# Two-layer transformer on one core: moving 32x32-square transposes of the MLP rows to VectorE

## The chip, the cores and the metric

The kernel runs on 1 core of one Trainium2 chip. The metric is device time in microseconds (us) of one launch; less is better. Engines are named as the profile names them: PE (TensorE, matrix multiply) with PEld (its weight loads), DVE (VectorE), ACT (ScalarE), POOL (GpSimd) and SP (the queue that issues most DMAs). Each engine works through its own instructions in order and waits on semaphores for the others.

## What is computed

Two equal layers, each an attention block and an MLP block, on one sequence of 2048 rows with 640 columns, all in fp32:

```python
x = x + A(layernorm(x))   # 32 heads of 20 columns: qkv = x @ wqkv, softmax(q k^T / sqrt(20)) v, then @ wo
x = x + B(layernorm(x))   # relu(x @ w1 + b1) ** 2 @ w2 + b2, with 1536 hidden columns
x = x + A(layernorm(x))
x = x + B(layernorm(x))
```

Each fp32 operand is split in a high part (rounded to PE's faster fp32r form) and a low part (the rest). A product is three matmuls: high x high, high x low, low x high (`THREE`, L284).

## The kernel before, in words

**Rows and blocks.** The 2048 rows are four blocks of 512 (`QB`), each block four row tiles of 128 rows x 640 columns. A matmul contracts over partitions, so the normalised rows must stand transposed: five tiles `xnT` of 128 columns (`k`) x 512 rows, high and low part side by side. Five tiles of 128 columns make the 640.

**How rows are transposed.** PE turns a 128x128 square by a matmul with the identity: twenty for a block, four into each of five PSUM banks. Then `split_to` (L265) makes the high part on ACT (L267, reads the bank) and the low part on DVE (L268), 128x512 each. This is done in `front` (L370, transposes at L385) for the attention's input and in `transposed` (L1037, transposes at L1042) for the MLP's.

**A layer.** `layer` (L1096) runs `qkv`, `attention`, then for each block `add_heads` (L1005: 8 chains of 15 matmuls with `wo`, each followed by a DVE add into the row tile, L1020), then for each block `mlp` (L1050).

**One MLP block.** `mlp` goes twice (`fh`) through the same two phases. The f phase has six hidden tiles: a chain of 15 matmuls of 128x512 on PE; relu with bias on ACT (L1065); the square on DVE (L1066); the split into `h` on ACT (L267) and DVE (L268). The y phase has eight chains (two column halves x four row tiles) of 18 matmuls of 128x320, each followed by a DVE add (L1085). The eight y chains need all six `h`. In the first f phase POOL also adds the bias `b2` to the four row tiles (L1072).

**What sets the order.** The order of each engine's instructions is the order in which the Python code issues them. Work for later is cut into generators, and `side()` (L1107), called after every chain, takes one step from the list `steps`:
- `normal_rows` (L1024) prepares the rows of the next block for `transposed`: one step of four loads on SP, four of statistics (`stats`, L250, DVE and two small POOL instructions, L258 and L259), four of `normalise` on DVE (L263).
- In an ordinary block these ten steps begin after six empty ones. `transposed` for the next block is called in the second y phase, after its third chain.
- For the first MLP block the ten steps are taken during the last `add_heads` block, and `transposed` follows it directly.
- In the last MLP block of the first layer the side steps are `ahead`: `second` (L1144), the `front` of the second layer's blocks 0, 1 and 2, three steps a call, from the first chain of the second f phase on; a `front` has 14 steps.

**Buffers.** Row tiles and the intermediate `r` share 11 buffers (`NX`), weights and `xnT`, `h` share 42 slots, PSUM has eight banks that `ps_all` hands out in turn, so PE can be eight chains ahead of whoever empties them.

Of the kernel before, what the change touches and what calls it, by code (L numbers as in the profile page):

```python
# [16 lines left out]
P = 128  # L17
# [7 lines left out]
QB = 512  # L25
# [14 lines left out]
def tile_layers(  # L40
# [221 lines left out]
    def normalise(eng, x, mv):  # L262
        eng.tensor_scalar(x, x, mv[:, 0:1], mv[:, 1:2], op0=ALU.subtract, op1=ALU.mult)  # L263
# [17 lines left out]
    def pool_lo(dst, a, b):  # L281
        nc.gpsimd.tensor_sub(dst, a, b)  # L282

    THREE = ((0, 0), (0, 1), (1, 0))  # L284

    def row_tile(src, r):
# [83 lines left out]
    def front(tb, x_src, bank):  # L370

        rows = [row_tile(x_src, tb * 4 + i) for i in range(4)]
        yield
        mvs = []
        for x in rows:
            mvs.append(stats(x))
            yield
        for x, mv in zip(rows, mvs):
            normalise(nc.vector, x, mv)
            yield  # L380
        res = []
        for k in range(KD):
            dst = bank("xt")
            for i in range(4):
                nc.tensor.transpose(  # L385
                    dst[:, i * P : (i + 1) * P], rows[i][:, k * P : (k + 1) * P], ident
                )
# [5 lines left out]
            yield  # L393

    def fronts(steps):

# [627 lines left out]
    def normal_rows(qb, x_src, res):  # L1024

        xs = [row_tile(x_src, qb * 4 + i) for i in range(4)]
        yield
        mvs = []
        for x in xs:
            mvs.append(stats(x))  # L1030
            yield
        for x, mv in zip(xs, mvs):
            normalise(nc.vector, x, mv)
            yield
        res.extend(xs)

    def transposed(xs):  # L1037
        xnt = []
        for k in range(KD):
            dst = ps_all("xt")  # L1040
            for i in range(4):
                nc.tensor.transpose(  # L1042
                    dst[:, i * P : (i + 1) * P], xs[i][:, k * P : (k + 1) * P], ident
                )
            t = slot([P, 2, QB], F32R, "xnT")
            split_to(t[:, 0, :], t[:, 1, :], dst)
            xnt.append(t)
        return xnt

    def mlp(qb, xnt, x_mid, x_dst, side, nxt):  # L1050

        xs, res = [], None
        for fh in range(2):
            hs = []
            for f in range(fh * 6, fh * 6 + 6):
                dst = ps_all("pu")
# [8 lines left out]
                nc.scalar.activation(r, dst, AF.Relu, bias=b1_t[:, f : f + 1])  # L1065
                nc.vector.tensor_mul(r, r, r)  # L1066
                h = slot([P, 2, QB], F32R, "h")
                split_to(h[:, 0, :], h[:, 1, :], r)
                hs.append(h)
                if fh == 0 and f in (1, 2, 3, 4):  # L1070
                    x = row_tile(x_mid, qb * 4 + f - 1)
                    nc.gpsimd.tensor_add(x, x, b2_t)  # L1072
                    xs.append(x)
                side()
            for hf in range(2):
                c = slice(hf * HALF, (hf + 1) * HALF)
                for i in range(4):
                    dst = ps_all("y")
                    chain(dst[:, :HALF], [
                        (hs[f % 6][:, hx, i * P : (i + 1) * P], w_2.piece(at_2(f, hw, hf)))  # L1080
                        for f in range(fh * 6, fh * 6 + 6)
                        for hx, hw in THREE
                    ])
                    x = xs[i]
                    nc.vector.tensor_add(x[:, c], dst[:, :HALF], x[:, c])  # L1085
                    if fh == 1 and hf == 1:
                        r0 = (qb * 4 + i) * P
                        dma(nc.sync, x_dst[r0 : r0 + P, :], x)
                    side()
                    if (fh, hf, i) == (1, 0, 2) and nxt:  # L1090
                        res = transposed(nxt)
            if fh == 0 and qb == NQB - 1:
                w_2.past(at_2(5, 1, 1))
        return res

    def layer(first, x_a, x_m, x_e, front_0, ahead):  # L1096
        qkv(first, x_a, front_0)
# [12 lines left out]

        def all_steps():
            while steps:
                side()

        for qb in range(NQB):
            if qb + 1 == NQB:
                rows = []
                norm = normal_rows(0, x_m, rows)
                steps.extend([lambda: next(norm, None)] * 10)
            add_heads(qb, x_a, x_m, xs, side)  # L1120
            for s in range(qb * 4, min(qb * 4 + 4, w_1.n)):
                w_1.load(s)
            if qb > 1:
                all_steps()
        w_o.drop()
        xnt = transposed(rows)
        for s in range(w_2.n):
            w_2.load(s)
        for qb in range(NQB):
            rows = []  # L1130
            if qb + 1 < NQB:
                norm = normal_rows(qb + 1, x_m, rows)
                steps.extend([None] * 6 + [lambda norm=norm: next(norm, None)] * 10)
            elif ahead:
                some = lambda: [next(ahead, None) for _ in range(3)]
                steps.extend([None] * 14 + [some] * 14)
            xnt = mlp(qb, xnt, x_m, x_e, side, rows if qb + 1 < NQB else None)
            if qb + 1 < NQB:
                all_steps()
        steps.clear()  # L1140
        w_1.drop()
        w_2.drop()

    def second():  # L1144

# [66 lines left out]
```

## Time and profile before

| what | value |
|---|---|
| median of the runs (lowest to highest) | 3760.36 us (3759.33 to 3761.38, 3 runs) |
| the profiled execution's own time | 3758.89 us |
| its span, first to last instruction | 3757.1 us |
| mean granted TensorE clock | 0.993 |
| PE busy | 3700.7 us, 98% of the span |
| DVE busy | 2788.9 us, 74% |
| ACT busy | 2554.5 us, 68% |
| POOL busy | 830.9 us, 22% |
| the eight MLP blocks | about 1537 to 1893 and 3409 to 3757 us of the span |

How to read it: busy time is an average over stages with different limits. In attention PE, DVE and ACT are all near full; in the MLP blocks the 40 slices of the page show DVE at four tenths and ACT at two. What a change in the MLP is worth is read there, from windows and timelines of that stretch, not from the averages.

### The profile page before, as it was taken

Reading aid. Unit: us, or ns where it says so; the run is one execution under the profiler, and the core shown is the slowest. Engines: PE = TensorE matmul, PEld = TensorE weight load, DVE = VectorE, ACT = ScalarE, POOL = GpSimd, SP = SyncE. Lnnn points to the kernel's source line nnn. Section 1 sums busy time; section 2 is a strip of 40 time slices with the busy share of each in tenths; the row PEclk is TensorE's granted clock in tenths of the full one; section 3 lists DMA queues with packets and bytes.
Section 4 is the critical chain, followed back from the end, with each engine's and each line's share of the span. In section 5 each row is a group of like instructions: output and inputs, shape, how many; then the busy total and the mean of one; then the engine's idle time right before and its main releaser. Section 6 shows DMA issues by size and latency. Waiting matters only on the chain.

```text
span 3757.1 us, 64225 instructions
## 1 busy us (share of the span) xinstructions
PE 3700.7 (98%) x23572; PEld 2121.8 (56%) x23572; DVE 2788.9 (74%) x4790; ACT 2554.5 (68%) x4887; POOL 830.9 (22%) x921
## 2 busy tenths in 40 slices
PE   7999999999999999999999999999999999999999
PEld 5667344333443336989866773344433344368998
DVE  7788999999999992444457879999999999814443
ACT  2454999999999995122214449999999999941211
POOL 6540234321112211111154201211221112101110
PEclk9999999999999999999999999999999999999999
DMA  7553554432212135511255543222222221365111
GB/s 223 185 205 133 130 155 148 138 104 67 65 48 60 44 93 192 222 43 43 95 168 182 160 141 83 77 67 64 70 73 56 54 54 43 99 217 191 43 46 39
DMA packets 258282, 405.87 MB, mean 108 GB/s; under 512 B 67828, under 2 KB 114676, under 8 KB 257968
## 3 DMA queue, kind: packets, MB, share of 16 engines
q1 hardware_dynamic: 257424, 400.06, 34.4%
q8 instruction: 186, 3.05, 0.3%
q10 hardware_dynamic: 544, 1.71, 0.2%
q14 instruction: 128, 1.05, 0.1%
HBM read 264.82 MB, written 136.81 MB: 107 GB/s over the span
## 4 chain that ended last, share of the span: by engine, by line
PE 92%; DMA 3%; DVE 2%; POOL 1%; ACT 1%; SPq 0%; issue 0%; ACTq 0%; DVEq 0%; POOLq 0%
PE banks L572 27%; PE banks L560 20%; PE banks L297 20%; PE banks L463 15%; PE banks L308 6%; PE banks L355 3%; DMA q<-d_qk 1%; DMA k<-d_qk 1%; PE banks L1042 0%; SPq L76 0%; DVE bst L255 0%; PE banks L385 0%; DVE h L268 0%; DVE r L1066 0%; POOL xnT L282 0%; DVE mx L484 0%
## 5 line engine op out<-in xcount | busy, mean ns | idle before, releaser
L567 ACT ACTIVATE e<-banks 128x512 f32<-128x512 f32 x4096 | 2113.9, 602 | 60.7 <-PE banks L560 4.4
L475 DVE TENSOR_REDUCE mx<-banks 128x1 f32<-128x512 f32 x2928 | 1839.4, 684 | 180.9 <-PE banks L463 112.8
L463 PE MATMUL banks<-k,q 60*128 60x512 f32 x3744 | 1153.2, 436 | 10.8 <-DMA q<-d_qk 7.8
L560 PE MATMUL banks<-q,k 62*128 62x512 f32 x4096 | 1151.7, 435 | 2.6 <-DVE mx L484 2.1
L572 PE MATMUL banks<-e,vg 128*32 128x512 f32 x8192 | 1092.1, 605 | 0.0
L560 PEld LDWEIGHTS banks<-q,k 62*128 62x128 f32 x4096 | 600.4, 185 | 701.2 <-ACT e L567 667.6
L463 PEld LDWEIGHTS banks<-k,q 60*128 60x128 f32 x3744 | 537.3, 185 | 337.3 <-DVE mx L475 204.2
L495 ACT ACTIVATE rl<-banks 128x512 f32<-128x512 f32 x352 | 191.6, 596 | 256.0 <-PE banks L463 255.9
L572 PEld LDWEIGHTS banks<-e,vg 128*32 128x32 f32 x8192 | 161.6, 108 | 358.5 <-issue 331.7
L297 PE MATMUL banks<-w,h 128*128 128x320 f32 x2304 | 352.7, 312 | 3.2 <-DVE h L268 2.7
L297 PEld LDWEIGHTS banks<-w,h 128*128 128x128 f32 x2304 | 340.8, 189 | 12.7 <-DVE h L268 6.9
L297 PE MATMUL banks<-xnT,w 128*128 128x512 f32 x1440 | 331.0, 390 | 0.0
L308 PE MATMUL banks<-xnT,wqk 128*128 128x512 f32 x1200 | 326.9, 416 | 1.1 <-POOL wqk L282 1.1
L1065 ACT ACTIVATE r<-banks,b_t 128x512 f32<-128x512 f32 x96 | 66.1, 689 | 381.1 <-PE banks L297 381.0
L505 DVE CUSTOM_DVE_ANT_0 rl<-banks,rl 128x512 f32<-128x512 f32 x352 | 229.2, 689 | 121.4 <-PE banks L463 116.3
L297 PEld LDWEIGHTS banks<-xnT,w 128*128 128x128 f32 x1440 | 270.1, 188 | 55.4
L484 DVE TENSOR_REDUCE mx<-banks 128x2 f32<-128x1024 f32 x232 | 279.6, 1221 | 25.6 <-PE banks L463 24.9
L308 PEld LDWEIGHTS banks<-xnT,wqk 128*128 128x128 f32 x1200 | 222.3, 195 | 87.4 <-issue 43.8
L616 POOL TENSOR_TENSOR few<-few,minus_t 128x16 f32<-128x16 f32 x62 | 179.9, 2902 | 226.3 <-DMA few<-d_s 223.0
L279 POOL CAST mr<-nt 128x32 fp32r<-128x32 f32 x64 | 13.5, 211 | 923.3 <-DVE nt L531 923.3
L1085 DVE TENSOR_TENSOR x<-banks,x 128x320 f32<-128x320 f32 x128 | 62.8, 491 | 200.8 <-PE banks L297 191.6
L627 POOL TENSOR_TENSOR o<-o 128x512 f32<-128x512 f32 x62 | 79.7, 1285 | 567.1 <-DMA o<-d_r 340.2
(73 smaller groups left out, 2000.9 us busy)
## 6 DMA issues: line engine op xcount, KB each, us to landing
q<-d_qk SPq DMA_DIRECT2D x756, 80.0 KB
d_qk<-ev SPq DMA_DIRECT2D x80, 512.0 KB
k<-d_qk SPq DMA_DIRECT2D x468, 80.0 KB
x<-d_x SPq DMA_DIRECT2D x96, 320.0 KB
d_o<-ot SPq DMA_DIRECT2D x248, 80.0 KB
ot<-d_o SPq DMA_DIRECT2D x38, 512.0 KB
d_v<-v SPq DMA_DIRECT2D x32, 512.0 KB
vg<-d_v SPq DMA_DIRECT2D x32, 512.0 KB
```

The source lines that it names most:

```text
L297: nc.tensor.matmul(dst, a, b, start=(n == 0), stop=(n == last))
L308: nc.tensor.matmul(dst, w_qk.piece(pos * 10 + hw * KD + k), xt_[tb][k][:, hx, :], start=(n == 0), stop=(n == 3 * KD - 1),)
L355: nc.tensor.matmul(dst[:, :HALF], xt_[tb][k][:, hx, i * P : (i + 1) * P], w_v.piece(k * 4 + hw * 2 + hf), start=(j == 0), stop=(j == 3 * K ...
L463: nc.tensor.matmul(dst, q_t[t][b : b + 60, p, sub * P : (sub + 1) * P], k_t[t // NQB, c][b : b + 60, p, :], start=True, stop=True,)
L475: nc.vector.tensor_reduce(maxima(t)[:, 2 * p + par, sub, c : c + 1], dst, axis=AX.X, op=ALU.max)
L484: nc.vector.tensor_reduce(maxima(t)[:, 2 * p : 2 * p + 2, sub, c], dst, axis=AX.X, op=ALU.max)
L495: nc.scalar.activation(res[par], dst[:, par, :], AF.Relu)
L505: nc.vector.tensor_tensor_reduce(out=r[par], in0=dst[:, par, :], in1=r[par], scale=1.0, scalar=LEAST, op0=ALU.add, op1=ALU.max, accum_out= ...
L560: nc.tensor.matmul(dst, k_t[t // NQB, kt // 4][b : b + 62, p, (kt % 4) * P : (kt % 4 + 1) * P], q_t[t][b : b + 62, p, :], start=True, stop ...
L567: nc.scalar.activation(es[p][:, par, :], dst, AF.Exp, scale=SCALE)
L572: nc.tensor.matmul(acc[32 * h : 32 * h + 32, :], v_t[t // NQB, kt // 8][:, kt % 8, 32 * h : 32 * h + 32], es[p][:, par, :], start=(kt == 0 ...
L616: nc.gpsimd.tensor_tensor(few, few, minus_t, op=ALU.pow)
```

## The change

Three things:

1. **Squares of 32 on DVE.** A new helper `turned` turns a 128x640 row tile into `y`, whose columns `k*128 ... k*128+127` are the transpose of the tile's k-th 128x128 square. It takes 16 `nc.vector.transpose` instructions; each reads 32 partitions x (5 x 32) elements and writes them, square by square, to 32 partitions x (5 x 32). It yields after eight and after sixteen. `parts` then makes the high part on ACT and the low part on POOL, in pieces of 128x128: five of each for a row tile. `transposed` and the fronts of the second layer's blocks 0 and 1 use these; the first layer's fronts and the second layer's blocks 2 and 3 stay on PE.
2. **Steps.** A block of `normal_rows` now has 14 steps instead of ten. For the first MLP block they begin one `add_heads` block earlier. `transposed` is called after the first chain of the second y phase instead of the third.
3. **The last block.** In the last MLP block of each layer, hidden tiles 0 to 3 of each half are squared on POOL and their low part is made there, instead of on DVE; tiles 4 and 5 stay.

```diff
+    def turned(x):
+        y = xtile("y")
+        view = y.rearrange("p (k t) -> p k t", k=KD)
+        src = x.rearrange("p (k c i) -> p c k i", k=KD, i=32)
+        for a in range(4):
+            for c in range(4):
+                nc.vector.transpose(
+                    view[32 * c : 32 * c + 32, :, 32 * a : 32 * a + 32],
+                    src[32 * a : 32 * a + 32, c],
+                )
+            if a % 2:
+                yield y
+
+    def parts(res, i, y):
+        for k, t in enumerate(res):
+            cols = slice(i * P, (i + 1) * P)
+            nc.scalar.copy(t[:, 0, cols], y[:, k * P : (k + 1) * P])
+            pool_lo(t[:, 1, cols], y[:, k * P : (k + 1) * P], t[:, 0, cols].bitcast(F32))
...
+    def front_turned(tb, x_src):
...
+        for i, mv in enumerate(mvs):
+            x = rows[i]
+            normalise(nc.vector, x, mv)
+            for y in turned(x):
+                yield
+            rows[i] = x = None
+            if not res:
+                res = [slot([P, 2, QB], F32R, "xnT") for _ in range(KD)]
+            parts(res, i, y)
+        xt_[tb] = res
+        yield
...
-        for x, mv in zip(xs, mvs):
-            normalise(nc.vector, x, mv)
-            yield
-        res.extend(xs)
-
-    def transposed(xs):
-        xnt = []
-        for k in range(KD):
-            dst = ps_all("xt")
-            for i in range(4):
-                nc.tensor.transpose(
-                    dst[:, i * P : (i + 1) * P], xs[i][:, k * P : (k + 1) * P], ident
-                )
-            t = slot([P, 2, QB], F32R, "xnT")
-            split_to(t[:, 0, :], t[:, 1, :], dst)
-            xnt.append(t)
+        for i, mv in enumerate(mvs):
+            normalise(nc.vector, xs[i], mv)
+            for y in turned(xs[i]):
+                yield
+            xs[i] = None
+            res.append(y)
+
+    def transposed(ys):
+        xnt = [slot([P, 2, QB], F32R, "xnT") for _ in range(KD)]
+        for i, y in enumerate(ys):
+            parts(xnt, i, y)
         return xnt
...
-                nc.vector.tensor_mul(r, r, r)
                 h = slot([P, 2, QB], F32R, "h")
-                split_to(h[:, 0, :], h[:, 1, :], r)
+                if qb < NQB - 1 or f % 6 > 3:
+                    nc.vector.tensor_mul(r, r, r)
+                    split_to(h[:, 0, :], h[:, 1, :], r)
+                else:
+                    nc.gpsimd.tensor_mul(r, r, r)
+                    nc.scalar.copy(h[:, 0, :], r)
+                    pool_lo(h[:, 1, :], r, h[:, 0, :].bitcast(F32))
...
-                    if (fh, hf, i) == (1, 0, 2) and nxt:
+                    if (fh, hf, i) == (1, 0, 0) and nxt:
...
-            if qb + 1 == NQB:
+            if qb + 2 == NQB:
...
-                steps.extend([lambda: next(norm, None)] * 10)
+                steps.extend([lambda: next(norm, None)] * 14)
...
-            if qb > 1:
+            if qb + 1 == NQB:
                 all_steps()
...
-                steps.extend([None] * 6 + [lambda norm=norm: next(norm, None)] * 10)
+                steps.extend([None] * 6 + [lambda norm=norm: next(norm, None)] * 14)
...
-        yield from front(0, d_x[1], ps_all)
-        for n, _ in enumerate(front(1, d_x[1], ps_all)):
+        yield from front_turned(0, d_x[1])
+        for n, _ in enumerate(front_turned(1, d_x[1])):
```

More of the change, by code (lines that the diff above doesn't have):

```diff
@@ L393, in front @@
             yield
+    def front_turned(tb, x_src):
+        rows = [row_tile(x_src, tb * 4 + i) for i in range(4)]
+        yield
+        mvs = []
+        for x in rows:
+            mvs.append(stats(x))
+            yield
+        res = []
+        for i, mv in enumerate(mvs):
[8 more added lines that the diff above has]
+        xt_[tb] = res
+        yield
     def fronts(steps):
@@ L1031, in normal_rows @@
             yield
-        for x, mv in zip(xs, mvs):
-            normalise(nc.vector, x, mv)
-            yield
-        res.extend(xs)
-    def transposed(xs):
-        xnt = []
-        for k in range(KD):
-            dst = ps_all("xt")
-            for i in range(4):
-                nc.tensor.transpose(
-                    dst[:, i * P : (i + 1) * P], xs[i][:, k * P : (k + 1) * P], ident
-                )
-            t = slot([P, 2, QB], F32R, "xnT")
-            split_to(t[:, 0, :], t[:, 1, :], dst)
-            xnt.append(t)
+        for i, mv in enumerate(mvs):
+            normalise(nc.vector, xs[i], mv)
+            for y in turned(xs[i]):
+                yield
+            xs[i] = None
[4 more added lines that the diff above has]
+            parts(xnt, i, y)
         return xnt
```

## Prediction

> **What bounds the kernel now.** I read the page's chain first, then windows over the MLP blocks, then the timelines of PE and DVE there.
>
> ```profile
> PE 92%; DMA 3%; DVE 2%; POOL 1%; ACT 1%; SPq 0%; issue 0%; ACTq 0%; DVEq 0%; POOLq 0%
> ```
>
> The chain that ends last is PE for 92% of the span. Whatever leaves PE there is time won; whatever makes PE wait is time lost. The windows (length, then busy time of PE, PEld, DVE, ACT, POOL, granted clock) show one ordinary block, its transposes, and the middle of the first layer's last block:
>
> ```profile
> 1611.00:1691.00 80.00, 79.63 (x439) 71.52 (x439) 34.06 (x57) 16.11 (x25) 10.93 (x12) 1.00 0.15 50
> 1691.00:1698.00 7.00, 7.00 (x55) 6.99 (x54) 2.83 (x6) 2.46 (x5) 0.00 (x0) 1.00 0.00 0
> 1843.00:1870.00 27.00, 24.88 (x117) 20.48 (x116) 17.80 (x36) 10.05 (x17) 3.89 (x8) 0.94 0.31 99
> ```
>
> An ordinary block leaves PE idle for 0.4 us of 80 while DVE has 46 us free, so moving transposes to DVE looks free. But the second f phase, where most of the new work goes, has to be read by itself. PE, the chain's piece for the transposes, then DVE:
>
> ```profile
> 1665.84 20.59 PE L297 MATMUL banks<-xnT,w 128*128 128x512 f32 x90
> 1686.27 2.94 PE L297 MATMUL banks<-w,h 128*128 128x320 f32 x17
> 1689.37 5.69 PE L297 MATMUL banks<-w,h 128*128 128x320 f32 x37 [0.16 <-DVE h L268]
> 1695.06 2.18 PE banks L1042 x20
> ```
>
> ```profile
> 1660.76 0.49 DVE L1085 TENSOR_TENSOR x<-banks,x 128x320 f32<-128x320 f32 x1 [1.11 <-PE banks L297]
> 1661.17 0.60 DVE L263 TENSOR_SCALAR x<-x,mv 128x640 f32<-128x640 f32 x1
> 1670.24 0.69 DVE L1066 TENSOR_TENSOR r<-r 128x512 f32<-128x512 f32 x1 [3.18 <-ACT r L1065]
> 1687.25 0.69 DVE L1066 TENSOR_TENSOR r<-r 128x512 f32<-128x512 f32 x1 [1.33 <-ACT r L1065]
> 1688.63 0.69 DVE L268 TENSOR_TENSOR h<-r,h 128x512 fp32r<-128x512 f32 x1 [0.69 <-ACT h L267]
> ```
>
> A hidden tile comes every 20.59/6 = 3.43 us. DVE holds 2.07 us of that in one piece (1687.25 to 1689.32: square, wait for ACT's copy, subtraction), leaving 1.36 us. Its last h lands at 1689.32, just as PE needs it: PE waits only 0.16 us. And the transposes that leave PE are worth just **2.18 us a block**.
>
> **The change part by part.** All hangs on T, the time from one 32x(5x32) transpose to the next. A block needs 64.
>
> ```profile
> L531 DVE STREAM_TRANSPOSE nt<-nm 128x32 f32<-128x32 f32 x64 | 13.6, 212 | 6.7 <-DVE nm L520 0.5
> L268 DVE TENSOR_TENSOR xnT<-banks,xnT 128x512 fp32r<-128x512 f32 x60 | 38.0, 685 | 13.5 <-ACT xnT L267 13.4
> 1536.05 3.08 DVE L268 TENSOR_TENSOR xnT<-banks,xnT 128x512 fp32r<-128x512 f32 x5 [1.09 <-ACT xnT L267]
> L171 ACT CAST wqk<-raw 128x128 fp32r<-128x128 f32 x2 | 0.6, 300 | 0.0
> L282 POOL TENSOR_TENSOR w<-raw,w 128x128 fp32r<-128x128 f32 x6 | 2.8, 460 | 0.2
> ```
>
> From this kernel's own rows: DVE's copy of a 128x320 bank into x takes 0.49 us and the 128x512 subtraction 0.685, so 192 elements cost 0.195 us, 1.02 ns each. The transpose of 32 elements takes 0.212 us: 0.18 fixed and 0.033 for elements. With 160 elements it is 0.18 + 0.163 = **0.345 us alone**. Five subtractions in a row took 3.08 us, (3.08 - 0.685)/4 = 0.60 apart: like neighbours overlap by 0.085 us, and all but 0.075 us of fixed cost can hide, so the lower estimate is 0.163 + 0.075 = **0.235 us**. Nothing shows less than 0.163 (elements alone) or excludes 0.48 (if each square of 32 is filled and emptied by itself, 0.18 - 0.033 + 10 x 0.033). I take 0.345: it is the nearest row, the same operation, taken whole, and each new transpose writes to other partitions than the one before, which the overlapping subtractions don't.
>
> The Trainium skill, "VectorE: DVE Perf Modes", section "Two Vector instructions with no wait between them", says that an instruction whose output starts in another group of 32 partitions than the last one starts only when all earlier ones have finished. The inner loop changes that group every time, so by it T is 0.345 and not 0.235; no row of this trace shows such a pair.
>
> *A. Six ordinary second f phases (blocks 0 to 2, both layers).* The changed order on DVE, from the sixth add of the first y phase (ends 1661.17 where the next instruction starts): four normalisations (0.61) and 64 transposes, with two adds (0.45) and six tiles (2.07) between: 2.44 + 64T + 0.90 + 12.42 = 15.8 + 64T. With 0.345 that is 37.8 us: the last h lands at 1699.0 instead of 1689.32, **9.7 us late**. DVE is busy throughout: it reaches tile 0's square at 1671.6, after 1670.24 when the relu was there. PE has finished the f phase at 1686.4 and stands in the first y chain; all later y chains are behind it in its order. Less 2.18 us of transposes: +7.5. Waiting costs more than the wait:
>
> ```profile
> 1874.07 0.33 PE L385 MATMUL banks<-ident,x 128*128 128x128 f32 x1 [1.84 <-DVE x L263]
> 1876.12 4.42 PE L297 MATMUL banks<-w,h 128*128 128x320 f32 x18
> 1881.62 2.88 PE L297 MATMUL banks<-w,h 128*128 128x320 f32 x18
> ```
>
> After a few idle microseconds the same 18 matmuls took 4.42 instead of 2.88 us, and the 1843:1870 window, with idle time, was granted 0.94. I add 1.5 us for each long stall. A is 6 x (7.5 + 1.5) = **+54**.
>
> The Trainium skill, "TensorE: Matmul & The Clock Gate", Part 1, has the clock at half rate after an idle window of about 3.4 us, until about as much time was busy; that makes 1.7 us a stall, and the sum would be about 2 us larger.
>
> The rest of an ordinary block costs nothing. `parts` is 20 copies on ACT (0.300, 6 us) and 20 subtractions on POOL (0.460, 9.2 us): both engines are idle in the second y phase, 21 us long (8 x 18 matmuls), of which seven chains are still to come; uncovered it would be 9 us. Five bank copies and subtractions leave ACT and DVE, hidden already. Number and order of DMAs are unchanged; rows that reuse y's buffers are loaded behind SP's stores of the block's output, later than `parts` ends.
>
> *B. The two entries to the MLP.* Here the rows are loaded behind the previous `add_heads` block's loads. SP, DVE and PE of the first layer:
>
> ```profile
> 1501.08 0.55 SPq L76 DMA_DIRECT2D x<-in_A_x_dram  x1
> 1518.71 2.53 SPq L76 DMA_DIRECT2D x<-d_x  x4
> 1525.92 0.89 DVE L255 BATCH_NORM_STATS2 bst<-x 128x6 f32<-128x320 f32 x2 [5.20 <-DMA x<-d_x]
> 1531.54 0.61 DVE L263 TENSOR_SCALAR x<-x,mv 128x640 f32<-128x640 f32 x1
> 1533.43 0.49 DVE L1020 TENSOR_TENSOR x<-banks,x 128x320 f32<-128x320 f32 x1 [0.36 <-PE banks L297]
> 1536.86 20.68 PE L297 MATMUL banks<-xnT,w 128*128 128x512 f32 x90
> ```
>
> Issue to data took 7.2 us (1518.71 to 1525.92); issued at about 1501.6 the rows are there at 1508.9. Statistics with four adds took 5.6 us: 1514.5. Then four normalisations, 64 transposes and seven adds (0.41), 5.3 + 22.1 us: 1541.9. The last row's copy and subtraction add 0.9: PE starts at 1542.8 and not at 1536.9, after standing from 1533.4. +5.9 and one slow start of 1.5, twice: **+15**. SP's later loads of w2 wait for the adds behind the transposes; they still lead their use by the same f phase.
>
> *C. The first layer's last block.* Its second f phase has two fronts on DVE: 128 transposes.
>
> ```profile
> 1842.85 0.69 ACT L1065 ACTIVATE r<-banks,b_t 128x512 f32<-128x512 f32 x1 [23.14 <-PE banks L297]
> 1846.76 0.19 POOL L258 TENSOR_TENSOR mv<-mv,eps_t 128x1 f32<-128x1 f32 x1 [37.34 <-DVE mv L256]
> 1847.03 0.55 POOL L259 TENSOR_TENSOR mv<-mv,half_t 128x1 f32<-128x1 f32 x1
> 1868.43 0.69 DVE L268 TENSOR_TENSOR h<-r,h 128x512 fp32r<-128x512 f32 x1 [0.69 <-ACT h L267]
> 1893.37 0.60 DVE L263 TENSOR_SCALAR x<-x,mv 128x640 f32<-128x640 f32 x1
> 1894.55 2.89 PE L297 MATMUL banks<-w,h 128*128 128x320 f32 x18
> 1898.55 9.38 PE L308 MATMUL banks<-xnT,wqk 128*128 128x512 f32 x40
> L282 POOL TENSOR_TENSOR xnT<-r,xnT 128x512 fp32r<-128x512 f32 x20 | 25.7, 1286 | 1.6
> ```
>
> The first normalisation needs POOL's `pow`, now behind POOL's square and subtraction of tile 0 (relu ends 1843.5, plus 1.29 + 0.69 + 1.29, plus 0.8 from 1846.76 to 1847.58): 1847.6. Three rows of 0.61 + 16 x 0.345: 1866.0; half a row more, 1869.4; tile 4: 1871.5; eight transposes, 1874.2. On ACT the fifth relu stands behind five copies that wait for these (1.5 us), then relu 0.7 and 2.07: the last h at **1878.5**, 9.4 later than 1869.1. Then DVE has, in order, 64 transposes of block 1, statistics ((5.6 - 1.6)/4 = 1.0 a row) and normalisations of blocks 1 and 2 and seven adds: 22.1 + 8.0 + 4.9 + 3.0, and 1.5 for POOL between, 39.5 us: 1918.0 for the normalisation that ended at 1894.0 before, and that PE's transposes of block 2 wait for, with the eighth y chain and the projections of the second layer behind them. +24, and one slow start: **+25**. The 40 PE transposes saved were inside these waits.
>
> *D. Squares on POOL.* POOL, ACT and POOL take 1.29 + 0.69 + 1.29 a tile, within 3.43. In the first half the b2 additions (8.02 us for four, row below) stand between; ACT's relus of tiles 4 and 5 then wait behind its copy of tile 3, and the last h comes about 1.5 us later. Second half without additions: nothing. Two layers: **+3** (0 to 5).
>
> ```profile
> 1801.40 8.02 POOL L1072 TENSOR_TENSOR x<-x,b_t 128x640 f32<-128x640 f32 x4 [54.17 <-DMA x<-d_x]
> ```
>
> **Sum:** 54 + 15 + 25 + 3 = +97 us on the profiled execution's 3758.9 (span 3757.1): 3856. The median of the runs is 1.5 us above it: **3857 us**.
>
> **The rivals.**
> *Neighbours overlap, T = 0.235.* 64 transposes are 7.0 us cheaper: A falls to 9.7 - 7.0 - 2.2 plus about 1 of slow clock, 6 x 1.5 = 9; B to 2 x -1, since PE's own end at 1533.4 and `parts` limit it; C to 25 - 14 = 11; D 3. +21: 3781. For it: the subtractions' spacing. Against: the changing partitions.
> *Faster: elements alone, T = 0.17.* This is the other side. Then the last h is set by the relu again, A is all gain, 6 x -2.2 = -13; B's rows are ready before PE ends, 2 x -3.5 = -7; C 25 - 22 = 3; D 3. -14: 3746. The place is DVE's second f phase; from about T = 0.20 down the gains outweigh C and D. Against it: no DVE row overlaps that far.
> *Squares filled and emptied one by one, T = 0.48.* 0.135 x 640 = 86 us more: 3943. The row of 32 elements can't exclude it.
>
> **How the numbers follow.** Forecast case (T 0.33 to 0.37) 0.65; overlap 0.20; faster 0.09; one by one 0.06. Each 0.01 us of T is 6.4 us; with the terms' errors the forecast case reaches from 3830 to 3885, the overlap case from 3768 to 3800. The range leaves out the two outer cases: 3770 to 3885. A difference of 0.2% (7.5 us) is about what a measurement of this kernel can tell from none. Faster by more 0.09; within 0.05, from the edges of overlap and faster; slower 0.86.
>
> **What would show each step.** A row for the transposes of about 0.345 us mean, 64 taking 22 us; PE waiting on DVE's h for about 10 us in each of six second f phases; PE waiting on POOL's xnT at both entries for 9 us; a wait of over 15 us at the last block's PE transposes; granted clock below 1.00 right after each. Wrong: transposes 0.24 us or less apart; PE released late by something else (a buffer, POOL's `parts`, DMAs of w2); or the six waits near zero.

## Result and profile after

The changed kernel takes 3867.97 us (median of 4 runs, 3865.04 to 3868.63) against 3760.87 us (4 runs, 3759.33 to 3761.62) for the kernel before: ratio 1.0282, 95% interval 1.0267 to 1.0298. It is slower by 107 us. The profiled execution of the changed kernel took 3867.35 us, its span is 3865.6 us, 108.5 us longer than before.

From the page of the changed kernel: the chain of work that ended last by engine, DVE's busy tenths in 40 slices, and the costliest groups of the MLP (busy us, mean ns of one, then the idle time before and what ended it).

```profile
PE 81%; DVE 9%; POOL 3%; issue 3%; DMA 2%; ACT 1%; SPq 0%; POOLq 0%; DVEq 0%; ACTq 0%
...
DVE  6787999999999964555477879999999999645551
...
L319 PE MATMUL banks<-w,h 128*128 128x320 f32 x2304 | 372.4, 321 | 74.4 <-ACT h L267 71.8
...
L319 PE MATMUL banks<-xnT,w 128*128 128x512 f32 x1440 | 333.6, 393 | 23.7 <-ACT xnT L303 23.7
...
L292 DVE STREAM_TRANSPOSE y<-x 32x160 f32<-32x160 f32 x640 | 215.1, 336 | 10.2
```

PE's share of the chain fell from 92 to 81%, and DVE's rose from 2 to 9%. PE's matmuls are the same, but those that read `h` now stand idle for 74.4 us in all, and those that read `xnT` for 23.7 us. The DVE slices of the MLP are still only half full (4 to 5 tenths): DVE is not full there on average, and yet it is what PE waits for. The 640 new transposes hold DVE for 215 us. The windows show where that matters: the second block of the first layer, from the start of its first f phase to the start of the next block's (length, then busy time and count of PE, PEld, DVE, ACT, POOL, granted clock, DMA share, GB/s), first before, then after.

```profile
1623.58:1710.28 86.70, 86.33 (x491) 78.21 (x490) 36.59 (x61) 18.27 (x29) 10.93 (x12) 1.00 0.14 46
```

```profile
1651.00:1747.11 96.11, 87.19 (x471) 78.09 (x470) 54.98 (x120) 19.21 (x44) 19.27 (x32) 0.95 0.13 42
```

One block with its next rows' preparation costs 9.4 us more, although PE has 20 instructions less to do and DVE is busy for only 55 of 96 us. The timeline of PE shows the second f phase and y phase of that block in the changed kernel (start, length, then in brackets the idle time before and its releaser):

```profile
1693.20 20.59 PE L319 MATMUL banks<-xnT,w 128*128 128x512 f32 x90
1713.63 1.48 PE L319 MATMUL banks<-w,h 128*128 128x320 f32 x9
1715.84 0.55 PE L319 MATMUL banks<-w,h 128*128 128x320 f32 x2 [0.73 <-ACT h L267]
1716.57 0.42 PE L319 MATMUL banks<-w,h 128*128 128x320 f32 x1 [0.17 <-DVE h L268]
1721.27 1.36 PE L319 MATMUL banks<-w,h 128*128 128x320 f32 x3 [4.29 <-ACT h L267]
1726.19 21.07 PE L319 MATMUL banks<-w,h 128*128 128x320 f32 x129 [3.56 <-ACT h L267]
1747.11 20.59 PE L319 MATMUL banks<-xnT,w 128*128 128x512 f32 x90
```

PE ran through its 90 matmuls of the f phase at the old pace, began the first y chain with the `h` that were there, and stood for 0.73 + 0.17 + 4.29 + 3.56 = 8.75 us for the last three. The bracket names ACT's copy as the releaser. DVE's timeline of the same moment shows who held ACT up:

```profile
1716.43 0.61 DVE L263 TENSOR_SCALAR x<-x,mv 128x640 f32<-128x640 f32 x1
1717.07 2.78 DVE L292 STREAM_TRANSPOSE y<-x 32x160 f32<-32x160 f32 x8
1719.88 0.69 DVE L1106 TENSOR_TENSOR r<-r 128x512 f32<-128x512 f32 x1
1721.25 0.69 DVE L268 TENSOR_TENSOR h<-r,h 128x512 fp32r<-128x512 f32 x1 [0.68 <-ACT h L267]
1721.98 2.79 DVE L292 STREAM_TRANSPOSE y<-x 32x160 f32<-32x160 f32 x8
...
1726.17 0.69 DVE L268 TENSOR_TENSOR h<-r,h 128x512 fp32r<-128x512 f32 x1 [0.68 <-ACT h L267]
```

DVE goes from one hidden tile to eight transposes to the next tile; it never waits but for ACT's 0.68 us inside a tile. The square (L1106) of each tile stands behind eight transposes, 2.78 us, and a tile with its transposes takes some 5 us, where PE makes one in 3.43. Eight transposes in 2.78 us are 0.3475 us apart, although the mean of one is 336 ns: none overlaps its neighbour.

### The profile page after: what moved, and what is told of

Read it like the earlier page. It is cut to its first block, busy times and chain, and to the rows that moved or that the text cites. A ratio compares the mean times of both kernels' runs of the same rounds, so it can differ in the third digit from the quotient of the medians.

```text
span 3865.6 us, 64832 instructions
## 1 busy us (share of the span) xinstructions
PE 3701.5 (96%) x23372; PEld 2114.4 (55%) x23372; DVE 2952.5 (76%) x5348; ACT 2566.3 (66%) x5037; POOL 951.9 (25%) x1153
## 4 chain that ended last, share of the span: by engine, by line
PE 81%; DVE 9%; POOL 3%; issue 3%; DMA 2%; ACT 1%; SPq 0%; POOLq 0%; DVEq 0%; ACTq 0%
PE banks L615 26%; PE banks L603 19%; PE banks L506 15%; PE banks L319 12%; PE banks L330 6%; DVE y L292 5%; PE banks L377 3%; DVE r L1106 1%; POOL xnT L282 1%; ACT h L267 1%; DVE x L263 1%; DVE h L268 1%; DMA q<-d_qk 1%; DMA k<-d_qk 1%; DVE bst L255 0%
## 5 line engine op out<-in xcount | busy, mean ns | idle before, releaser
L319 PE MATMUL banks<-w,h 128*128 128x320 f32 x2304 | 372.4, 321 | 74.4 <-ACT h L267 71.8
L319 PEld LDWEIGHTS banks<-w,h 128*128 128x128 f32 x2304 | 355.6, 196 | 90.9 <-ACT h L267 79.6
L319 PE MATMUL banks<-xnT,w 128*128 128x512 f32 x1440 | 333.6, 393 | 23.7 <-ACT xnT L303 23.7
L292 DVE STREAM_TRANSPOSE y<-x 32x160 f32<-32x160 f32 x640 | 215.1, 336 | 10.2
```

The source lines that it names most:

```text
L292: nc.vector.transpose(view[32 * c : 32 * c + 32, :, 32 * a : 32 * a + 32], src[32 * a : 32 * a + 32, c],)
L319: nc.tensor.matmul(dst, a, b, start=(n == 0), stop=(n == last))
```

## Experiments

### The transpose by itself: fewer instructions, and other partitions

**e1.** Each row tile turned by two instructions over all 128 partitions, not by sixteen over 32.

```diff
-        for a in range(4):
-            for c in range(4):
-                nc.vector.transpose(
-                    view[32 * c : 32 * c + 32, :, 32 * a : 32 * a + 32],
-                    src[32 * a : 32 * a + 32, c],
-                )
-            if a % 2:
-                yield y
+        for h in range(2):
+            cols = slice(h * HALF, (h + 1) * HALF)
+            nc.vector.transpose(y[:, cols], x[:, cols])
+            yield y
```

> What it is: every group of eight 32-partition transposes is replaced by one transpose of 128 partitions x 320, which turns each square of 32 in its own partitions (the squares aren't brought to their places, so this leaves out part of the computation; everything else stays: the copies on ACT, the subtractions on POOL, the steps, the squares on POOL). Theory (DVE's time for the transposes makes the last h, the entries and the last block late): one such instruction should take about 0.18 + 0.33 = 0.5 us instead of 8 x 0.345 = 2.8, so a block needs 4 us of DVE instead of 22 and fits in the gaps; the six blocks then gain the 2.2 us of PE transposes each (-13), the entries 3.5 each (-7), the last block is about as before (-5 to +2), POOL's squares still cost 4 to 5: about 3743 us, between 3735 and 3755. Rival (ACT, POOL, buffers or DMAs of the new path make PE late, DVE only looks busy): the time stays above 3830 us.

Measured: 3738.57 us (3735.24 to 3740.28, 4 runs), ratio 0.9947 (0.9933 to 0.9962) to the kernel before (3758.31 on that chip). The group of its transposes:

```profile
L290 DVE STREAM_TRANSPOSE y<-x 128x320 f32<-128x320 f32 x80 | 39.9, 504 | 4.7 <-POOL h L282 3.4
```

The same squares of 32, in 80 instructions and not 640, take 39.9 us of DVE instead of 215. With that alone the kernel goes from 107 us slower to 20 us faster. So ACT's and POOL's pieces of 128x128, POOL's squares, the buffers and the new steps are not what costs 107 us by themselves: PE's matmuls that read `h` stand idle for 12.9 us in e1, not 74.4, and what is left includes the wait for POOL's squares (term D below). And one instruction over four times the partitions and twice the columns costs 0.504 us, where one of 160 columns on 32 partitions costs 0.336: the time goes by elements per partition, and the changed kernel lets 96 of 128 partitions rest in each of its 640 instructions.

**e2.** Each transpose reads the partitions that it writes, and four of them in a row stay there.

```diff
-        for a in range(4):
-            for c in range(4):
+        for c in range(4):
+            for a in range(4):
                 nc.vector.transpose(
                     view[32 * c : 32 * c + 32, :, 32 * a : 32 * a + 32],
-                    src[32 * a : 32 * a + 32, c],
+                    src[32 * c : 32 * c + 32, a],
                 )
-            if a % 2:
+            if c % 2:
```

> What it is: the same 640 transposes of 32x(5x32), but each reads and writes the same group of 32 partitions, and four follow each other in one group before it changes (the squares aren't brought to their places, so part of the computation is left out). Theory (a transpose waits for the end of the one ahead because the group of partitions changes): three of four now overlap and come 0.235 to 0.26 us apart, mean about 0.27; at 6.4 us for each 0.01 us the time is about 3868 - 48 = 3820 us, between 3805 and 3830. Rival (a transpose takes 0.345 us from start to start by itself, whatever the partitions): 3868 us as the changed kernel.

Measured: 3815.84 us (3809.02 to 3819.63, 4 runs), ratio 1.0152 (1.0137 to 1.0167). The group, and from DVE's timeline two sets of eight:

```profile
L292 DVE STREAM_TRANSPOSE y<-x 32x160 f32<-32x160 f32 x640 | 162.8, 304 | 3.5
```

```profile
1684.09 2.04 DVE L292 STREAM_TRANSPOSE y<-x 32x160 f32<-32x160 f32 x8
...
1688.26 2.06 DVE L292 STREAM_TRANSPOSE y<-x 32x160 f32<-32x160 f32 x8
```

Eight now take 2.05 us, 0.256 us each, with the same number of instructions of the same shape. That is a mean: the fifth of the eight still changes partitions. One by one in the trace, the second of a group of partitions starts 0.27 us after the first and the next two 0.226 us apart, while the first of the other group starts 0.30 us after the one ahead, which has then ended. So neighbours do overlap when the partitions stay, and the rival's price of 0.235 was right for them (0.24 on average); only, the changed kernel never gives it that case.

**e3.** The two loops exchanged alone: four in a row write the same partitions, and what they read still moves.

```diff
-        for a in range(4):
-            for c in range(4):
+        for c in range(4):
+            for a in range(4):
...
-            if a % 2:
+            if c % 2:
```

> What it is: the changed kernel with its two transpose loops exchanged: the group of partitions written stays for four transposes, the group read changes with each. The same result, the same count. Theory in its full form (a change of the group read holds an instruction back as a change of the group written does): no difference, 3868 us, transposes 0.345 us apart. Rival (only the group written matters): three of four overlap, 3820 us as in the experiment with the same partitions on both sides. Second rival (partitions don't matter at all): 3868 us in both.

Measured: 3865.6 us (3865.44 to 3865.69, 4 runs), ratio 1.0286 (1.0269 to 1.0303), the changed kernel's own time.

```profile
L292 DVE STREAM_TRANSPOSE y<-x 32x160 f32<-32x160 f32 x640 | 215.0, 336 | 10.2
```

A change of the read partitions alone holds the next instruction as well as a change of both. The Trainium skill, "VectorE: DVE Perf Modes", section "Two Vector instructions with no wait between them", states it so: a start partition group other than the last one read or the last one written is enough. The runs agree: 0.226 to 0.27 us apart without a change (e2), 0.35 with one (e3 and the changed kernel). A square that has to move from partition group a to c changes one of the two at each step, so no order of these loops helps.

### The terms of the sum

**e4.** Only the six ordinary blocks as in the changed kernel; entries, fronts and squares as before.

```diff
-                if qb < NQB - 1 or f % 6 > 3:
+                if True:
...
-            if qb + 2 == NQB:
+            if qb + 1 == NQB:
                 rows = []
-                norm = normal_rows(0, x_m, rows)
-                steps.extend([lambda: next(norm, None)] * 14)
+                norm = rows_pe(0, x_m, rows)
+                steps.extend([lambda: next(norm, None)] * 10)
...
-            if qb + 1 == NQB:
+            if qb > 1:
                 all_steps()
         w_o.drop()
-        xnt = transposed(rows)
+        xnt = transposed_pe(rows)
...
-        yield from front_turned(0, d_x[1])
-        for n, _ in enumerate(front_turned(1, d_x[1])):
+        yield from front(0, d_x[1], ps_all)
+        for n, _ in enumerate(front(1, d_x[1], ps_all)):
```

`rows_pe` and `transposed_pe` are the kernel before's `normal_rows` and `transposed`, on PE.

> What it is: of the change only step A: the six ordinary blocks' rows are turned on DVE; the entries to the MLP, the second layer's fronts and all squares are as before. Theory (the terms add up, and the six second f phases cost 9.6 us each as the trace of the changed kernel shows): 3761 + 58 = 3819 us, between 3812 and 3826. Rival (the stalls in the blocks come partly from the other parts of the change, which shift DMAs and buffers): clearly less, under 3805 us.

Measured: 3813.36 us (3812.39 to 3814.17, 4 runs), ratio 1.0147 (1.0132 to 1.0162): +55 us for A alone, nearly what the sum has for it. The blocks' loss doesn't hang on the other parts of the change.

**e5.** The changed kernel with the second layer's fronts on PE.

```diff
-        yield from front_turned(0, d_x[1])
-        for n, _ in enumerate(front_turned(1, d_x[1])):
+        yield from front(0, d_x[1], ps_all)
+        for n, _ in enumerate(front(1, d_x[1], ps_all)):
```

> What it is: the changed kernel with the second layer's fronts back on PE; blocks, entries and squares on POOL stay changed. Theory (C: 128 transposes on DVE put the last block's PE transposes off by 25 us): 3867 - 25 = 3842 us, between 3836 and 3848. Rival (what puts them off is POOL: its squares stand ahead of the pow that each normalisation waits for): the squares are still there, so less than 12 us come back, over 3855.

Measured: 3839.73 us (3834.95 to 3845.01, 4 runs), ratio 1.0216 (1.0203 to 1.0229). That is 28 us less than the changed kernel, or 25.6 less when each is set against the kernel before of its own runs (81.5 us above 3758.28, 107.1 above 3760.87). PE's timeline at the last y chains, e5 first, then the changed kernel:

```profile
1935.67 0.75 PE L407 MATMUL banks<-ident,x 128*128 128x128 f32 x3
1937.01 0.77 PE L407 MATMUL banks<-ident,x 128*128 128x128 f32 x5 [0.59 <-DVE x L263]
...
1941.48 9.35 PE L330 MATMUL banks<-xnT,wqk 128*128 128x512 f32 x40
```

```profile
1887.56 20.59 PE L319 MATMUL banks<-xnT,w 128*128 128x512 f32 x90
1907.99 2.06 PE L319 MATMUL banks<-w,h 128*128 128x320 f32 x12
1920.50 1.36 PE L319 MATMUL banks<-w,h 128*128 128x320 f32 x3 [10.46 <-ACT h L267]
1927.34 18.53 PE L319 MATMUL banks<-w,h 128*128 128x320 f32 x111 [5.48 <-ACT h L267]
1964.27 1.52 PE L407 MATMUL banks<-ident,x 128*128 128x128 f32 x3 [18.39 <-DVE x L263]
...
1972.02 9.37 PE L330 MATMUL banks<-xnT,wqk 128*128 128x512 f32 x40
```

PE waits 18.39 and 0.45 us for DVE's normalisations of block 2 in the changed kernel; when the 128 transposes of the fronts are not in front of them, the first of the two waits is gone and the second is 0.59 us. Since e5 keeps POOL's squares, POOL's place ahead of the `pow` can't have been the cause, as the rival had it.

**e6.** The squares of the last blocks back on DVE, the rest as in the changed kernel.

```diff
-                if qb < NQB - 1 or f % 6 > 3:
+                if True:
```

> What it is: the changed kernel with all squares back on DVE; everything else changed. Theory: the first halves of the two last blocks win back D, 2.35 us each by the changed kernel's trace (-4.7); in the second half of the first layer's last block four tiles of 2.07 us now stand between the transposes on DVE, the last h comes about 8 us later (+8): 3867 + 3.5 = 3871 us, between 3867 and 3876. Rival (POOL's squares only cost): 3863 us.

Measured: 3870.1 us (3868.07 to 3872.5, 4 runs), ratio 1.0298 (1.0283 to 1.0313). The intervals of this ratio and of the changed kernel's, 1.0282 (1.0267 to 1.0298), overlap, so the times don't settle the sign of the squares on POOL. The trace does. In the first layer's last block, PE's first half takes 42.20 us in e6 and 44.60 in the changed kernel, 2.4 less, and the second layer's the same; the second half of the first layer takes 92.61 us and not 84.46, 8.15 more. So POOL's squares cost 4.8 us where DVE has time and save 8.15 where it is late, as expected.

### Can DVE turn the rows for nothing?

If all of it is DVE's time at the wrong moment, the same transposes must be free where DVE has room for them and nobody waits for their end.

**e7.** The kernel before, with the rows of four ordinary blocks and both entries turned on DVE by the changed kernel's own instructions, 384 of them, spread over earlier sides. The rows of each layer's block 1, the fronts and the squares stay as before.

```diff
-            if qb + 1 == NQB:
+            if qb == 1:
                 rows = []
                 norm = normal_rows(0, x_m, rows)
-                steps.extend([lambda: next(norm, None)] * 10)
+                step = lambda: next(norm, None)
+                steps.extend([step] + [None] * 5 + [step] * 4 + [step, step, None] * 4 + [step])
...
-                norm = normal_rows(qb + 1, x_m, rows)
-                steps.extend([None] * 6 + [lambda norm=norm: next(norm, None)] * 10)
+                norm = (normal_rows if qb else rows_pe)(qb + 1, x_m, rows)
+                step = lambda norm=norm: next(norm, None)
+                if qb:
+                    steps.extend([None] + [step] * 11 + [None] * 8 + [step] * 3)
+                else:
+                    steps.extend([None] * 6 + [step] * 10)
```

> What it is: DVE's transposes only where DVE has room. The rows of the first MLP block are loaded in the second add_heads block, and their steps spread over the second to fourth; for blocks 2 and 3 six of the eight half tiles are turned in the first y phase and the last two in the second y phase, none in the second f phase; block 1 of each layer, all fronts and all squares are as in the kernel before. Theory (what costs is where DVE's 22 us stand, not that they exist): four blocks gain the 2.18 us of PE transposes each (-8.7), two entries gain up to 3.5 each (-7): 3759 - 16 = 3743 us, between 3740 and 3750, faster than both kernels. Rival (the transposes cost PE time wherever they stand, by buffers, by ACT and POOL or by DVE's adds coming late): 3760 us or more.

Measured: 3757.83 us (3753.71 to 3765.83, 11 runs), ratio 1.0003 (0.9993 to 1.0013). The loss is gone, but the gain of 16 us didn't come. PE's timeline of e7 at the first entry and in the first half of the second block, the first whose next rows DVE turns; then DVE's and one line of POOL's ahead of the second wait; last, one line each of POOL and DVE in the same half of the kernel before:

```profile
1540.41 22.61 PE L319 MATMUL banks<-xnT,w 128*128 128x512 f32 x90 [2.20 <-ACT xnT L303]
...
1653.57 0.56 PE L319 MATMUL banks<-w,h 128*128 128x320 f32 x2 [1.66 <-ACT h L267]
```

```profile
1645.11 1.80 DVE L268 TENSOR_TENSOR h<-r,h 128x512 fp32r<-128x512 f32 x1 [0.69 <-ACT h L267]
1646.84 0.88 DVE L255 BATCH_NORM_STATS2 bst<-x 128x6 f32<-128x320 f32 x2
...
1649.20 2.07 DVE L268 TENSOR_TENSOR h<-r,h 128x512 fp32r<-128x512 f32 x1 [0.69 <-ACT h L267]
```

```profile
1644.80 1.57 POOL L1141 TENSOR_TENSOR x<-x,b_t 128x640 f32<-128x640 f32 x1
```

```profile
1628.09 7.96 POOL L1072 TENSOR_TENSOR x<-x,b_t 128x640 f32<-128x640 f32 x4 [54.23 <-DMA x<-d_x]
1634.73 1.86 DVE L1066 TENSOR_TENSOR r<-r 128x512 f32<-128x512 f32 x1
```

Two misses. At the entry the last transposes ended 1.8 us after PE's last chain; PE waited 2.20 us and then ran its first f phase in 22.61 instead of 20.59 us, so that nothing was won. In the blocks the statistics, which I had moved to the first f phase to make room, met POOL's additions of `b2`: the last two additions now stand behind POOL's share of the statistics and run beside the fourth and fifth hidden tile. DVE's subtractions beside them took 1.80 and 2.07 us and not 0.69, the last `h` came late and PE waited 1.66 us. The kernel before has the same clash (its square above took 1.86 us), but beside the first three tiles, and DVE has caught up by the last. A block that gives PE 2.18 us and takes 1.7 back shows no gain.

**e8.** Of e7 the entries alone, so that the two misses can be told apart.

```diff
-                        res = (transposed if qb else transposed_pe)(nxt)
+                        res = transposed_pe(nxt)
...
-                norm = (normal_rows if qb else rows_pe)(qb + 1, x_m, rows)
-                step = lambda norm=norm: next(norm, None)
-                if qb:
-                    steps.extend([None] + [step] * 11 + [None] * 8 + [step] * 3)
-                else:
-                    steps.extend([None] * 6 + [step] * 10)
+                norm = rows_pe(qb + 1, x_m, rows)
+                steps.extend([None] * 6 + [lambda norm=norm: next(norm, None)] * 10)
```

> What it is: the spread kernel with only the two entries on DVE, all blocks' rows turned by PE as before. Theory: up to 3.5 us an entry, 3759 - 7 = 3752 us, between 3750 and 3757; the difference to the spread kernel is then the four blocks' 8.7 us. Rival (PE waits at the entry for ACT's and POOL's last pieces as long as it waited for its own transposes): no gain, 3759 us.

Measured: 3759.2 us (3754.46 to 3767.54, 12 runs), ratio 1.0003 (0.9995 to 1.0012), with the same 2.20 us of idle PE at the first entry. A miss again: the entry gains nothing as long as DVE's end comes after PE's.

**e9.** The kernel of e7 with both mended: the entry's work two sides earlier and without gaps, the blocks' statistics in the first y phase, half of the transposes in each y phase.

```diff
-                steps.extend([step] + [None] * 5 + [step] * 4 + [step, step, None] * 4 + [step])
+                steps.extend([step] + [None] * 3 + [step] * 13)
...
-                    steps.extend([None] + [step] * 11 + [None] * 8 + [step] * 3)
+                    steps.extend([None] + [step] + [None] * 4 + [step] * 8 + [None] * 6 + [step] * 5)
...
-                    if (fh, hf, i) == (1, 0, 2) and nxt:
+                    if (fh, hf, i) == ((1, 1, 0) if qb else (1, 0, 2)) and nxt:
```

> The kernel of e7 with its work laid out by the two misses that its trace shows. Entries: the four statistics two sides earlier and the eight half tiles in eight sides without gaps, so that the last transposes end about 5 us ahead of PE's last chain (they ended 1.8 us behind it). Blocks: rows loaded in the first f phase, statistics in the first y phase behind its rows' b2 sums, two tiles turned in the first y phase, two in the second. Theory (a transpose costs VectorE 0.35 us and PE nothing, so that it is free where VectorE has 0.35 us to spare for each and its end is not waited for): PE's 2.18 us of transposes go in four blocks and its 3.46 us of idle time in two entries, 3758 - 4*2.18 - 2*3.46 = 3743 (3740 to 3748). Rival (a busy VectorE always makes PE wait somewhere, or PE's clock and its matmuls pay for what the transposes had cost): 3756 or more, as e7.

Measured: 3742.32 us (3739.88 to 3748.86, 6 runs) against 3757.8 (16 runs), ratio 0.9965 (0.9953 to 0.9977). PE's timeline of e9 at the first entry and in the second half of the second block, and DVE's at the end of the entry's transposes:

```profile
1467.26 68.76 PE L319 MATMUL banks<-wo,ot 128*128 128x320 f32 x465
1535.86 20.59 PE L319 MATMUL banks<-xnT,w 128*128 128x512 f32 x90
...
1664.82 20.59 PE L319 MATMUL banks<-xnT,w 128*128 128x512 f32 x90
...
1688.36 18.89 PE L319 MATMUL banks<-w,h 128*128 128x320 f32 x127 [0.17 <-DVE h L268]
1707.08 20.59 PE L319 MATMUL banks<-xnT,w 128*128 128x512 f32 x90
```

```profile
1529.70 2.79 DVE L292 STREAM_TRANSPOSE y<-x 32x160 f32<-32x160 f32 x8
```

```profile
L292 DVE STREAM_TRANSPOSE y<-x 32x160 f32<-32x160 f32 x384 | 129.0, 336 | 6.1
```

The transposes cost DVE what they cost it in the changed kernel, 336 ns each, 129 us in all, and PE sees nothing of them. At the entry they end at 1532.5, PE's chains at 1536.0, and the f phase follows without a gap. The block's second half has no wait but the old 0.17 us, and lasts 42.26 us where it lasted 44.4.

**e10.** Of e9 the blocks alone; the entries as in the kernel before.

```diff
-            if qb == 1:
+            if qb + 1 == NQB:
                 rows = []
-                norm = normal_rows(0, x_m, rows)
-                step = lambda: next(norm, None)
-                steps.extend([step] + [None] * 3 + [step] * 13)
+                norm = rows_pe(0, x_m, rows)
+                steps.extend([lambda: next(norm, None)] * 10)
...
-        xnt = transposed(rows)
+        xnt = transposed_pe(rows)
```

> The blocks of e9 alone, the entries as in the kernel before. Theory: 3758 - 4*2.18 = 3749 (3747 to 3752), and so 6 us above e9. Rival (VectorE's 22 us in these blocks cost PE waits as long as its own transposes): 3757 to 3760.

Measured: 3750.01 us (3743.35 to 3753.38, 11 runs), ratio 0.9978 (0.9969 to 0.9987): 7.8 us from four blocks (8.7 expected), and so 7.7 us of e9 from the two entries (6.9 expected).

## Why the prediction was right, step by step

The forecast was 3857 us and slower; the time is 3867.97. The mechanism is shown: DVE takes 0.35 us for each of 640 transposes (e1, e2), between hidden tiles that PE waits for (the timelines), and without that clash 384 of them at the same price cost nothing (e9). All four terms came out larger than forecast, by 10.7 us together; none made up for another.

**T.** Predicted 0.345 us alone; measured 0.3475 apart. The working was a fixed 0.18 us and 1.02 ns an element; it also gives 0.18 + 0.33 = 0.51 us for e1's 320 elements, measured 0.504. (The row of 0.49 us that it uses is an add from a bank, not a copy; the 1.02 ns holds all the same.) So squares of 32 are not filled and emptied one by one, and that rival falls. The two rivals with overlap fall by e3, and e2 shows how close the nearer one was: 0.24 us between neighbours if the partitions had stayed.

**A, six ordinary blocks.** Predicted +54; in the timelines the six second f and y phases are longer by 9.2 to 10.2 us, 57.7 in all, and e4 has 55 by itself. In the block shown above, the last `h` is 10.2 us late and not 9.7: it lands 33.66 us after the f phase began (1726.17 + 0.69 - 1693.20), and landed after 23.48 before. But the sum took the whole delay for PE's wait, and two sizes in it were off, in opposite directions. The wait was 8.75 - 0.16 = 8.6 us, since PE works between the tiles and takes up the last one before its low part is there. The slow clock cost more than the 1.5 us that I took: the y phase's 144 matmuls lasted 33.48 - 8.75 = 24.73 us, and before they lasted 24.0 less 2.18 for the transposes and 0.16 of waiting, 21.67; that is 3.06 us. The windows of the changed kernel show it (columns as above):

```profile
1713.63:1726.19 12.56, 3.81 (x16) 2.48 (x14) 10.13 (x26) 3.08 (x6) 0.00 (x0) 0.75 0.00 0
1726.19:1729.69 3.50, 3.50 (x12) 3.27 (x13) 1.17 (x2) 3.50 (x19) 3.27 (x8) 0.50 0.00 0
1729.69:1747.11 17.42, 17.42 (x119) 17.42 (x119) 2.95 (x6) 0.44 (x3) 5.43 (x13) 0.99 0.15 57
```

In the 3.50 us after the last wait PE was granted a clock of 0.50, and did 12 matmuls where 119 later took 17.42 us. The Trainium skill, "TensorE: Matmul & The Clock Gate", Part 1, has half rate after an idle window and for about 3.4 us of work, and the row of 3.50 us at 0.50 agrees; but the block had two long waits in a row, 4.29 and 3.56 us, and I had priced one. That 9.7 + 1.5 came so near to 8.6 + 3.06 is luck in part.

**B, two entries.** Predicted +15; measured 20.2, the largest error in a term. PE stood for 12.82 us in the first layer (PE's timeline of the changed kernel), where it had lost 3.46 before (1533.40 to 1536.86), and the first f phase took 22.39 instead of 20.68 us: +9.4 and +1.7; the second layer gave +6.8 and +2.3. SP's queue, DVE and PE of the changed kernel:

```profile
1508.09 3.15 SPq L76 DMA_DIRECT2D x<-d_x  x4
```

```profile
1517.96 0.89 DVE L255 BATCH_NORM_STATS2 bst<-x 128x6 f32<-128x320 f32 x2 [8.45 <-DMA x<-d_x]
```

```profile
1471.02 68.76 PE L319 MATMUL banks<-wo,ot 128*128 128x320 f32 x465
1552.61 22.39 PE L319 MATMUL banks<-xnT,w 128*128 128x512 f32 x90 [12.82 <-ACT xnT L303]
```

The step that failed in the first layer is "issue to data took 7.2 us": issued where predicted (1508.09 here; this stretch lies 6.4 us later than in the trace of before), the rows came after 9.87 us. That is 2.7 us of the excess; two of the normalisations at 0.77 to 0.78 instead of 0.61 us and the gaps between instructions make about one more. In the second layer they came no later than 7.5 us after their issue, and the excess is smaller there. Why the DMA was slower was not tried. The bracket names ACT's copy as what ends the wait, and not POOL's subtraction as forecast. Behind both waits the f phase lost more than the 1.5 us of one slow start.

**C, the first layer's last block.** Predicted +25, measured 1972.02 - 1887.56 = 84.46 us for its second half against 1898.55 - 1839.22 = 59.33 before: +25.1. With the fronts on PE again, e5, that half takes 56.55 us. The last `h` was predicted 39.3 us into that half (1878.5 - 1839.2), and PE goes on at 1927.34, 39.8 us into it.

**D, squares on POOL.** Predicted +3; measured +2.35 in each layer's first half, 4.7. The wait was foreseen, on ACT's copy; the 1.5 us for it should have been 2.2. What the squares save in the second half (e6) is part of C, which was forecast with them on POOL. The last line is POOL's group of squares in the changed kernel; one was costed at 1.29 us, as its subtractions, and took 1.04:

```profile
1868.09 0.56 PE L319 MATMUL banks<-w,h 128*128 128x320 f32 x2 [2.18 <-ACT h L267]
```

```profile
L1109 POOL TENSOR_TENSOR r<-r 128x512 f32<-128x512 f32 x16 | 16.7, 1042 | 84.3 <-ACT r L1103 84.3
```

**`parts` for nothing.** Right: ACT's 200 copies (294 ns) and POOL's 200 subtractions (480 ns) are in the changed kernel's groups, and e1, with the same pieces, is 20 us faster than before.

```profile
L303 ACT CAST xnT<-y 128x128 fp32r<-128x128 f32 x200 | 42.0, 294 | 178.2 <-DVE y L292 178.2
...
L282 POOL TENSOR_TENSOR xnT<-y,xnT 128x128 fp32r<-128x128 f32 x200 | 89.0, 480 | 300.4 <-ACT xnT L303 300.4
```

**Sum.** 57.7 + 20.2 + 25.1 + 4.7 = 107.7 of the 108.5 us between the two spans. The rest is no part of the change: the first layer's `add_heads` begins 6.4 us later than before (1471.02 against 1464.64) with nothing changed ahead of it, and the second layer's attention is 5.3 us shorter; that start lies at 1464 to 1471 us in the profiled executions of these kernels.

## What to carry to other kernels

An engine that is half idle on average can still be the one that ends last: before work is given to it, take the interval between two results that the bound engine waits for (3.43 us here), subtract what the engine holds in it (2.07) and compare the piece that will stand in front (2.78). The same work pays when it is put where the slack is larger than the piece, and when its end comes before the bound engine's own: 107 us lost became 15 us won with the same instruction at the same price, 384 of the 640 of them. Count a VectorE transpose by its elements per partition: the form that uses 32 of 128 partitions has four times as many for the same data, and took 215 us here against 39.9 (e1).

## What the runs showed of the hardware beside that

- Transposes of 32x160 with no wait between them start 0.226 to 0.27 us apart when neither the read nor the written group of partitions changes, and 0.35 us apart when either does at each step (e2, e3, the changed kernel).
- Waits of PE can cost more than they last: between and behind 8.75 us in four pieces, 3.06 us were lost, at a granted clock of 0.50 behind the last. A wait of 2.20 us was followed by an f phase of 22.61 instead of 20.59 us, with a granted clock of 0.64 in its first 3.1 us (e7). But the wait of 2.18 us in D was followed by matmuls at their full pace (127 in 18.91 us, 18.89 before) at a granted clock of 1.00, so the length of a wait alone doesn't tell.
- DVE's subtractions and squares of 128x512 that began while a POOL addition of 128x640 ran ended 0.55 us after it, whenever they had begun: 1.80 and 2.07 us in e7, 1.25 to 1.86 in the second block of the kernel before, 0.69 otherwise. DVE's statistics and its adds from a bank took no longer beside such an addition (0.49 us for an add of 128x320). Which of their accesses collide was not tried.
